# The third chunk's first layer norm regrouped through memory and turned by VectorE instead of TensorE

## The chip, the cores and the metric

The kernel runs on one core of a Trainium2 chip, in one launch. The metric is the device time of that core in microseconds (us). Times of a profile are counted from the start of the profiled span.

## The reference

The kernel computes one adaLN block over 2048 tokens of width 512, in float32: a linear attention with 32 heads of width 16, and a bilinear feed-forward of width 1376, each behind a layer norm that a condition vector scales and shifts.

```python
def _layernorm(x, eps=1e-5):
    m, v = mean(x, -1), var(x, -1)
    return (x - m) / jnp.sqrt(v + eps)

mod = (silu(c) @ w_mod)                      # six parts of 512: sa, ca, ga, sb, cb, gb
h = _layernorm(x) * (1 + ca) + sa
x = x + ga * A(h, wqkv, wo)
h = _layernorm(x) * (1 + cb) + sb
x = x + gb * (((h @ w_gate) * (h @ w_up)) @ w_down)

def A(x, wqkv, wo):
    q, k, v = heads(x @ wqkv)
    phi = lambda t: jnp.where(t > 0, t + 1, jnp.exp(t)) + 1e-6
    pq, pk = phi(q), phi(k)
    kv, z = sum_s(pk * v), sum_s(pk)         # per head: a 16 x 16 matrix and a vector
    return merge((pq @ kv) / (pq @ z + 1e-6)) @ wo
```

## The kernel before

A matrix product in float32 is made of three matmuls in a rounded format: each operand x is split into a high part h (a cast, on ACT) and a low part l = x - h (a subtraction, on DVE), and h*h, h*l and l*h are summed in PSUM. So each operand of a product costs a cast and a subtraction of a 128x512 tile.

The 2048 tokens are four chunks of four tiles of 128 tokens: tile i is tile j of chunk ch, i = 4 ch + j. The order of all instructions is written out by hand; each engine runs its own in that order, and semaphores make one engine wait for another. SBUF is a ring of 94 tiles of 128x512 (`B`), PSUM has four banks for accumulators (`acc_bank`) and four for work (`bank`). All DMAs are issued from the queue of SyncE (SP).

The first stage is the loop over i from 0 to 15 (L525 to L587). In step i, PE makes the keys of tile i + 2 (`proj(i + 2, wk)`, 12 matmuls), in the steps of `q_at` (i = 3, 4, 6, 7) also a query projection (`proj(..., wq)`, 12 matmuls) of one of the first four tiles, and the products of tile i's keys with its normalized tokens (`t_tile`, 12 matmuls into four accumulators). Beside that ACT and DVE split the normalized tile i + 1 (`k_split_x`) and its keys (`k_split`), apply phi to the keys of tile i + 2 (`k_phi`: two passes on ACT, one on DVE) and to the queries (`q_a`, `q_b`), and add up z (`z_add`).

The first layer norm of chunk ch + 1 (class `Norm`; `nx` in the loop) is spread over the steps of chunk ch and the end of the chunk before: the statistics of two tiles at j = 2 and two at j = 3 on DVE, the inverse deviation on POOL (`rstd_of`, a power) and `nmr_of` on DVE, then the scaled tile n on ACT (`xhat`; two tiles at j = 3, the others at j = 0 of the next chunk). At j = 0 and j = 1 of the chunk `turn_at` has `turn_x`: PE transposes the 128x128 blocks of the four tiles n into PSUM banks (L293, eight in each of the two steps), and `modulated` scales and shifts each bank on ACT (f, L305), casts it on DVE (L313) and subtracts (L316). The four pairs (h, l) of `norm[ch].t` are the left operands of the keys and queries of that chunk. For chunk 3 (index 2) this is in steps 4 and 5, and its first keys are made in step 6; for chunk 4 (index 3) it is in steps 8 and 9.

A second way to turn a tile is in use in later stages: a tile goes to DRAM and comes back with its 32x32 blocks regrouped, and DVE's transpose of 32x32 blocks does the rest. `move_out` and `move_in` do it for queries (one DMA out, four in, L723 and L731), `flip` and `flipped` for the second layer norm of the last two chunks, with the constant buffer `wide` between them (L901, L907).

The dictionary `extra` has the work on weights and modulation that is hung on the steps: the splits of the value weights in steps 4 to 7, the modulation from step 6 on, and the splits of the output weights `raw_o` in steps 12 and 13. Behind the loop come `den_z`, the scaling and splitting of the four accumulators (L655, L656, L660), and their product with the value weights (128x128 matmuls of `product` into `kvps`).

Of the kernel before, what the change touches and what calls it, by code (L numbers as in the profile page):

```python
# [8 lines left out]
F32 = mybir.dt.float32  # L9
F32R = mybir.dt.float32r  # L10
AF = mybir.ActivationFunctionType
ALU = mybir.AluOpType
AX = mybir.AxisListType

P = 128
NB = 94
BL = 32
NQ = P // BL
# [6 lines left out]
def tile_adaln_block(  # L25
# [42 lines left out]
    def f32(ap):  # L68
        return ap.bitcast(F32)
# [7 lines left out]
    def B(tag, shape=(P, D), dt=F32):  # L77

        return T(tiles, tag, shape, dt)
# [4 lines left out]
    def bank():  # L84
        return T(ps_w, "bank")
# [80 lines left out]
    def mod_col(acc, ps):  # L166

        for b in range(KD):
            nc.tensor.matmul(ps[:, b:b + 1], acc[:, b * P:(b + 1) * P], ones[:, 0:1], start=True, stop=True)
        return ps  # L170

    def col_out(v, ps, add):
        t = consts.tile([P, KD], F32, name=f"col{v}")
        nc.vector.tensor_scalar(t, ps[:, :KD], add, None, op0=ALU.add)
        return t
# [17 lines left out]
    def split(src, h, l, low=None):  # L193
        nc.scalar.activation(h, src, AF.Copy)  # L194
        (low or nc.vector).tensor_tensor(l, src, f32(h), op=ALU.subtract)  # L195

    def split_raw(raw, shape=(P, D), low=None):
        h = B("w", shape, F32R)
        l = B("w", shape, F32R)
        split(raw, h[:raw.shape[0]], l[:raw.shape[0]], low)  # L200
        return h, l
# [17 lines left out]
    def by_row(x):  # L219
        return x.rearrange("p (q s i) -> p s q i", q=NQ, i=BL)  # L220

    def split_blocks(raw):
        h, l = B("w", dt=F32R), B("w", dt=F32R)
        view = lambda x: x.rearrange("p (q s i) -> p q s i", q=NQ, i=BL)
        nc.scalar.activation(view(h), by_block(raw), AF.Copy)
        nc.vector.tensor_tensor(view(l), by_block(raw), view(f32(h)), op=ALU.subtract)
        return h, l
# [89 lines left out]
                self.t[k] = (h, l)  # L317


    NT = NCH * NJ  # L320
    norm = [Norm(xts[0])]
    wk, wq, wv = [], [], []
# [2 lines left out]
    def proj(i, w, of=bank):  # L325

        ch, j = divmod(i, NJ)
        ps = of()
        rows = w is wq and i not in FLIPPED
        product(ps.rearrange("p (s q i) -> p s q i", q=NQ, i=BL) if rows else ps,  # L330
                [(cut(norm[ch].t[k], j * P, (j + 1) * P), tuple(by_row(x) for x in w[k]) if rows else w[k])
                 for k in range(KD)])
        return ps
# [9 lines left out]
    def k_split_x(i):  # L343
        ch, j = divmod(i, NJ)
        kx[i] = [B("xh", dt=F32R), B("xl", dt=F32R)]
        split(norm[ch].n[j], *kx[i])

    def k_phi(i, ps):
        phi = B("phi")
# [11 lines left out]
    def k_split(i):  # L361
        h, l = B("kh", dt=F32R), B("kl", dt=F32R)
        phi = phk[i]
        nc.scalar.activation(h, phi, AF.Identity, bias=eps_phi)
        nc.vector.scalar_tensor_tensor(l, phi, EPS_PHI, f32(h), op0=ALU.add, op1=ALU.subtract)
        kx[i] += [h, l]

    def t_tile(i, *ks):
        xh, xl, kh, kl = kx[i]
        first, last = i == 0, i == NT - 1  # L370
        for k in ks:
            a, b = k * P, (k + 1) * P
            nc.tensor.matmul(tacc[k], xh[:, a:b], kh, start=first, stop=False)  # L373
            nc.tensor.matmul(tacc[k], xl[:, a:b], kh, start=False, stop=False)  # L374
            nc.tensor.matmul(tacc[k], xh[:, a:b], kl, start=False, stop=last)  # L375
# [6 lines left out]
    def q_b(i):  # L382
        phi_b(q_ps.pop(i), phq[i])
# [117 lines left out]
    def mod_load(*vs):  # L501
        raw_m.update({v: load_mod(v) for v in vs})

    def mod_part(v, *ks):
        if 0 in ks:
            accs[v] = B("f")
        mod_acc(accs[v], raw_m[v], ks)
# [6 lines left out]
             9: lambda: (mod_part(2, 2, 3), mod_load(4)),  # L514
             10: lambda: (pairs.update({2: split_raw(accs[2], low=nc.gpsimd)}), mod_part(3, 0, 1, 2), raw_o.extend(load(wo_v[k], "raw") for k in range(2))),
             11: lambda: (mod_part(3, 3), mod_part(4, 0, 1), rows.update({2: mod_row(2, pairs[2])}), raw_o.extend(load(wo_v[k], "raw") for k in range(2, KD))),
             12: lambda: (mod_part(4, 2, 3), wo_s.extend(split_raw(x) for x in raw_o[:2]), cols.update({3: col_out(3, mod_col(accs[3], bank()), 0.0)}), mod_load(5)),
             13: lambda: (mod_part(5, 0, 1, 2), wo_s.extend(split_raw(x) for x in raw_o[2:]), cols.update({4: col_out(4, mod_col(accs[4], bank()), 1.0)})),
             14: lambda: (mod_part(5, 3),)}
    pairs = {}  # L520
    q_at = {3: 0, 4: 1, 6: 2, 7: 3}
    ahead = {2: k_ps[2], 3: k_ps[3]}
    turn_at = {4 * ch + j: (ch + 1, 2 * j, 2 * j + 1) for ch in range(1, NCH - 1) for j in range(2)}
    turn_at.update({1: (1, 0, 1), 2: (1, 2, 3)})
    for i in range(NT):  # L525
        ch, j = divmod(i, NJ)
        done = 0
        if i > 2:
            ahead[i + 2] = proj(i + 2, wk) if i + 2 < NT else proj(i + 6 - NT, wq)
        if i in q_at:  # L530
            qps = proj(q_at[i], wq)
        def turn_x():
            to, *ks = turn_at[i]
            nx.transpose(*ks)
            nx.modulated(ca, sa, *ks, cast=nc.vector)
            norm[to:] = [nx]

        fresh = i > 0 and ch + 1 < NCH and j == 0
        if i == 2:
            turn_x()  # L540
            wq.extend(split_blocks(r) for r in raw_q)
        if fresh:
            nx.xhat(2)
        if 0 < i < NT - 1:
            k_split_x(i + 1)
        if fresh:
            nx.xhat(3)
        if 0 < i < NT - 1:
            k_split(i + 1)
        if i in turn_at and i != 2:  # L550
            t_tile(i, 0, 1)
            done = 2
            turn_x()
        if i == 2:
            t_tile(i, *range(KD))
            done = KD
            ahead[i + 2] = proj(i + 2, wk)
        if ch + 2 < NCH and j == 2:
            nx2 = Norm(xts[ch + 2])
            nx2.stats(0, 1)  # L560
        if ch + 2 < NCH and j == 3:
            nx = nx2
            nx.stats(2, 3)
            nx.rstd_of()
            nx.nmr_of()
            nx.xhat(0, 1)
        if i + 2 < NT:
            k_phi(i + 2, ahead.pop(i + 2))
        else:
            q_a(i + 6 - NT, ahead.pop(i + 2))  # L570
            q_b(i + 6 - NT)
        if i in q_at:
            q_a(q_at[i], qps)
            q_b(q_at[i])
        if i + 1 < NT:
            z_add(i + 1)
        if i == NT - 2:
            pairs["z"] = split_raw(zacc, low=nc.gpsimd)
        if i == NT - 1:
            zps = row_sum(pairs["z"])  # L580
            zb = consts.tile([P, D], F32, name="zb")
            nc.scalar.activation(zb, zps, AF.Identity, bias=eps_z)
            zq = B("z")
            nc.gpsimd.tensor_copy(zq.rearrange("p (q s i) -> p q s i", q=NQ, i=BL), by_block(zb))
        t_tile(i, *range(done, KD))
        if i in extra:
            extra[i]()  # L587
    ga, sb, cb = rows[2], cols[3], cols[4]
# [114 lines left out]
    def turn_h(i):  # L703
        pqs[i] = (B("xh", dt=F32R), B("xl", dt=F32R))
        nc.scalar.activation(pqs[i][0], tps[i], AF.Copy)
# [13 lines left out]
    def move_out(*tiles):  # L719

        for i in tiles:
            moved[i] = tc.dram_tile([P, D], F32, name=f"moved_{i}")
            nc.sync.dma_start(moved[i], phq.pop(i))  # L723

    def move_in(*tiles):

        for i in tiles:
            v = moved[i].rearrange("(m i) (q c) -> q i m c", i=BL, c=P)
            moved[i] = B("u")
            for q in range(NQ):  # L730
                nc.sync.dma_start(moved[i][q * BL:(q + 1) * BL].rearrange("i (m c) -> i m c", c=P), v[q])  # L731

    def turn_v(i):

# [19 lines left out]
    def y_seed(i, of=acc_bank):  # L754

        yps[i] = of()
        nc.scalar.activation(yps[i], xts[i // NJ][i % NJ], AF.Copy)
# [140 lines left out]

    def flip(ch, *js):
        for j in js:  # L900
            nc.vector.transpose(wide[:, j].rearrange("p (m s i) -> p m s i", m=NQ, i=BL),  # L901
                                blocks.pop((ch, j)).rearrange("p (m s i) -> p m s i", m=NQ, i=BL))

    def flipped(ch, *ks):
        for k in ks:
            f = B("f")
            nc.scalar.activation(f.rearrange("p (x i) -> p x i", i=BL),  # L907
                                 wide.rearrange("p j (m s i) -> p (j m) s i", m=NQ, i=BL)[:, :, k],
                                 AF.Identity, scale=cb[:, k:k + 1], bias=sb[:, k:k + 1])
            blocks[ch, "f", k] = f  # L910

    stowed, blocks = {}, {}

# [403 lines left out]
    first[0].sum("s1", "s3", on=nc.gpsimd)  # L1317
    g(lambda: turn_v(13))
    y_seed(13, y_bank)
    norm2[2].xhat_blocks(2, 3)  # L1320
    turn_h(13)
    turn_l(13)
    move_in(14, 15)
    stow(2, 0, 1, 2, 3)
# [107 lines left out]
```

## Time and profile before

| | |
|---|---|
| median of 3 runs | 554.86 us (554.34 to 554.95) |
| the profiled run | 554.37 us |
| its span | 552.7 us |
| granted TensorE clock | 1.000 |
| PE busy | 547.0 us (99%), 2488 matmuls |
| DVE busy | 373.6 us (68%) |
| ACT busy | 291.7 us (53%) |
| POOL busy | 203.4 us (37%) |
| DMA | 58.28 MB, mean 105 GB/s |

PE is the matmuls of TensorE, DVE is VectorE, ACT is ScalarE, POOL is GpSimd. A row of the timeline gives the start in us, the duration in us, the engine, the line of the kernel, the operation, out<-in by the program's names, the shapes and the count; in brackets stands the idle time ahead of it and what ended that. A row of the groups gives the line, engine, operation, names and shapes with their count, then the busy time in us and the mean ns of one, then the idle time before them. A row of the stretches gives the busy us of PE, the weight loads (PEld), DVE, ACT and POOL in turn, then the granted clock, the DMA share and GB/s.

### The profile page before, as it was taken

To read this page: it belongs to the slowest core of one execution; us is meant where nothing else is said; L and a number is where in the kernel's file an instruction comes from. 1 tells how busy PE (TensorE), PEld (TensorE's weight loads), DVE (VectorE), ACT (ScalarE), POOL (GpSimd) and SP (SyncE) were. 2 spreads that over 40 slices of the span, in tenths; PEclk is the share of its full clock that TensorE was granted. 3 is DMA by queue.
4 is the path that set the end of the run, shared out by engine and by line. 5 is a ranking of instruction groups with operands and counts; after the bars stand their busy time and mean duration, and the time that the engine had idled before them with its cause. 6 is when DMAs were issued, how large, how long until landed. Compare 5 with 4: busy or idle time off the path is not lost.

```text
span 552.7 us, 7324 instructions
## 1 busy us (share of the span) xinstructions
PE 547.0 (99%) x2488; PEld 449.2 (81%) x2488; DVE 373.6 (68%) x610; ACT 291.7 (53%) x539; POOL 203.4 (37%) x204
## 2 busy tenths in 40 slices
PE   8999999999999999999999999999999999999997
PEld 7788888888888878878888888877888888888886
DVE  7896968986887886778776576985444444434434
ACT  3695856646476667566684545454443444444110
POOL 2000000102003201057596666766666546446200
PEclk9999999999999999999999999999999999999999
DMA  8900203320503205845545071690434222200004
GB/s 284 387 15 2 76 20 103 108 77 1 157 2 133 96 5 186 267 145 135 160 111 155 0 230 38 216 322 2 133 116 132 59 57 59 58 20 0 1 0 152
DMA packets 58373, 58.28 MB, mean 105 GB/s; under 512 B 7328, under 2 KB 38304, under 8 KB 58336
## 3 DMA queue, kind: packets, MB, share of 16 engines
q1 hardware_dynamic: 58336, 57.83, 33.2%
q8 instruction: 19, 0.31, 0.2%
q14 instruction: 18, 0.15, 0.1%
HBM read 42.60 MB, written 15.20 MB: 105 GB/s over the span
## 4 chain that ended last, share of the span: by engine, by line
PE 99%; DVE 0%; issue 0%
PE bank L1030 33%; PE acc L766 7%; PE acc L1110 6%; PE acc L1111 6%; PE acc L1112 6%; PE bank L207 5%; PE bank L209 5%; PE bank L208 5%; PE acc L375 3%; PE acc L374 3%; PE acc L373 3%; PE bank L849 2%; PE bank L851 2%; PE bank L850 2%; PE acc L146 2%; PE bank L293 2%
## 5 line engine op out<-in xcount | busy, mean ns | idle before, releaser
L1030 PE MATMUL bank<-h,w 128*128 128x512 f32 (+1 forms) x798 | 184.7, 390 | 0.0
L1030 PEld LDWEIGHTS bank<-h,w 128*128 128x128 f32 (+1 forms) x798 | 148.4, 186 | 33.4 <-ACT bank L1035 0.7
L1035 ACT ACTIVATE bank<-bank 128x512 f32<-128x512 f32 (+1 forms) x38 | 22.2, 583 | 139.6 <-PE bank L1030 139.5
L836 DVE TENSOR_TENSOR x<-acc,x 128x512 f32<-128x512 f32 (+1 forms) x73 | 48.8, 682 | 48.4 <-PE acc L1112 47.7
L1016 POOL TENSOR_TENSOR w<-raw,w 128x256 fp32r<-128x256 f32 (+3 forms) x38 | 40.9, 1077 | 91.0 <-ACT w L1009 91.0
L1111 PE MATMUL acc<-w,kh 128*128 128x512 f32 (+2 forms) x154 | 59.6, 387 | 0.0
L1110 PE MATMUL acc<-w,kh 128*128 128x512 f32 (+2 forms) x154 | 59.6, 387 | 0.0
L1112 PE MATMUL acc<-w,kl 128*128 128x512 f32 (+2 forms) x154 | 59.5, 386 | 0.0
L263 POOL TENSOR_TENSOR rstd<-ve,half 128x4 f32<-128x4 f32 (+1 forms) x10 | 11.0, 1103 | 121.8 <-DVE ve L262 69.6
L195 POOL TENSOR_TENSOR w<-raw,w 128x512 fp32r<-128x512 f32 (+1 forms) x25 | 35.1, 1409 | 52.2 <-ACT w L194 47.3
L1016 POOL TENSOR_TENSOR w<-t,w 128x512 fp32r<-128x512 f32 (+1 forms) x38 | 49.2, 1318 | 0.0
L195 DVE TENSOR_TENSOR kl<-u,kh 128x512 fp32r<-128x512 f32 (+1 forms) x38 | 26.4, 736 | 30.6 <-ACT kh L194 30.6
L207 PE MATMUL bank<-w,h 128*128 128x512 f32 x104 | 40.9, 394 | 0.0
L209 PE MATMUL bank<-w,h 128*128 128x512 f32 x104 | 40.6, 391 | 0.0
L208 PE MATMUL bank<-w,h 128*128 128x512 f32 x104 | 40.6, 390 | 0.0
L766 PE MATMUL acc<-w,xh 128*128 128x512 f32 x120 | 37.4, 393 | 0.0
L1089 DVE TENSOR_TENSOR u<-bank,u 128x512 f32<-128x512 f32 (+1 forms) x19 | 13.1, 691 | 31.6 <-PE bank L1030 25.1
L1110 PEld LDWEIGHTS acc<-w,kh 128*128 128x128 f32 (+1 forms) x154 | 28.9, 188 | 6.0
L1112 PEld LDWEIGHTS acc<-w,kl 128*128 128x128 f32 (+1 forms) x154 | 28.9, 188 | 5.9
L1111 PEld LDWEIGHTS acc<-w,kh 128*128 128x128 f32 (+1 forms) x154 | 28.9, 188 | 5.9
L998 POOL TENSOR_TENSOR t<-raw,t 128x256 f32<-128x256 f32 (+1 forms) x34 | 25.9, 761 | 1.4
L766 PEld LDWEIGHTS acc<-w,xh 128*128 128x128 f32 x120 | 22.2, 188 | 4.6
(211 smaller groups left out, 1116.5 us busy)
## 6 DMA issues: line engine op xcount, KB each, us to landing
raw<-in_w_mod_dram SPq DMA_DIRECT2D x24, 256.0 KB, 3.7
raw<-in_B_w_down_dram SPq DMA_DIRECT2D x20, 256.0 KB, 3.2
raw<-in_B_w_gate_dram SPq DMA_DIRECT2D x36, 128.0 KB, 3.4
raw<-in_B_w_up_dram SPq DMA_DIRECT2D x36, 128.0 KB, 3.4
x<-in_A_x_dram SPq DMA_DIRECT2D x16, 256.0 KB, 5.4
out_dram<-x SPq DMA_DIRECT2D x15, 256.0 KB, 2.6
raw<-in_A_wqkv_dram SPq DMA_DIRECT2D x12, 256.0 KB, 5.4
moved<-h SPq DMA_DIRECT2D x12, 256.0 KB, 2.1
```

The lines of the kernel that those rows point to most:

```text
L195: (low or nc.vector).tensor_tensor(l, src, f32(h), op=ALU.subtract)
L207: nc.tensor.matmul(ps, ah, bh, start=i == 0, stop=False)
L208: nc.tensor.matmul(ps, ah, bl, start=False, stop=False)
L209: nc.tensor.matmul(ps, al, bh, start=False, stop=i == n - 1)
L766: nc.tensor.matmul(yps[i], x, y, start=False, stop=k == KD - 1 and x is al, skip_group_check=True)
L836: nc.vector.tensor_tensor(xt[:, a:b], dn[j][:, a:b], xt[:, a:b], op=ALU.add)
L998: sub = lambda out, x, y: (on or nc.gpsimd).tensor_tensor(out, x, y, op=ALU.subtract)
L1016: sub = lambda out, x, y: (on or nc.gpsimd).tensor_tensor(out, x, f32(y), op=ALU.subtract)
L1030: mm = lambda x, y, **kw: nc.tensor.matmul(ps, x[:, k], y, skip_group_check=True, **kw)
L1110: nc.tensor.matmul(ps, hh[:, a:b], dh[:n, c:d], start=i == 0, stop=False)
L1111: nc.tensor.matmul(ps, hh[:, a:b], dl[:n, c:d], start=False, stop=False)
L1112: nc.tensor.matmul(ps, hl[:, a:b], dh[:n, c:d], start=False, stop=i == len(hs) - 1)
```

## The change

For chunk 3 alone (`LIFTED = (2,)`) the 16 transposes on PE go. Its statistics, `nmr` and scaled tiles n are made in pairs, all by the end of step 3, with the columns of n grouped in blocks (`xhat_blocks`). Each n goes to DRAM (`lift_out`, one DMA) and back regrouped (`lift_in`, four DMAs), DVE turns it into `wide` (`lift_turn`: two tiles at the end of step 4, two in step 5), ACT scales and shifts four rows out of `wide` (`lift_row`), and the parts are made by `lift_parts`, the cast on ACT for rows 0 and 2 and on DVE for rows 1 and 3. `k_split_x` reads that chunk's n through a permuting pattern. In step 6 the query projection goes ahead of the keys of tile 8, the first that need chunk 3. The splits of the output weights move from steps 12 and 13 to steps 14 and 15. In a later stage `turn_h(13)` goes ahead of two scaled tiles of the second norm. `move_out`, `move_in`, `flip` and `flipped` call the new helpers and do the same as before.

```diff
+    LIFTED = (2,)
+
+    def lift_out(name, x):
+        to = tc.dram_tile([P, D], F32, name=name)
+        nc.sync.dma_start(to, x)
+        return to
+
+    def lift_in(of):
+        v = of.rearrange("(m i) (q c) -> q i m c", i=BL, c=P)
+        u = B("u")
+        for q in range(NQ):
+            nc.sync.dma_start(u[q * BL:(q + 1) * BL].rearrange("i (m c) -> i m c", c=P), v[q])
+        return u
+
+    def lift_turn(j, u):
+        nc.vector.transpose(wide[:, j].rearrange("p (m s i) -> p m s i", m=NQ, i=BL),
+                            u.rearrange("p (m s i) -> p m s i", m=NQ, i=BL))
+
+    def lift_row(k, scale, shift):
+        f = B("f")
+        nc.scalar.activation(f.rearrange("p (x i) -> p x i", i=BL),
+                             wide.rearrange("p j (m s i) -> p (j m) s i", m=NQ, i=BL)[:, :, k],
+                             AF.Identity, scale=scale[:, k:k + 1], bias=shift[:, k:k + 1])
+        return f
+
+    def lift_parts(k, f, cast=True):
+        h, l = B("h", dt=F32R), B("h", dt=F32R)
+        if k % 2 and cast:
+            nc.vector.tensor_copy(h, f)
+        else:
+            nc.scalar.activation(h, f, AF.Copy)
+        nc.vector.tensor_tensor(l, f, f32(h), op=ALU.subtract)
+        return h, l
...
-        split(norm[ch].n[j], *kx[i])
+        if ch not in LIFTED:
+            split(norm[ch].n[j], *kx[i])
+            return
+        x = by_row(norm[ch].n[j])
+        h, l = (t.rearrange("p (s q i) -> p s q i", q=NQ, i=BL) for t in kx[i])
+        nc.scalar.activation(h, x, AF.Copy)
+        nc.vector.tensor_tensor(l, x, f32(h), op=ALU.subtract)
...
-             12: lambda: (mod_part(4, 2, 3), wo_s.extend(split_raw(x) for x in raw_o[:2]), ...
-             13: lambda: (mod_part(5, 0, 1, 2), wo_s.extend(split_raw(x) for x in raw_o[2:]), ...
-             14: lambda: (mod_part(5, 3),)}
+             12: lambda: (mod_part(4, 2, 3), ...
+             13: lambda: (mod_part(5, 0, 1, 2), ...
+             14: lambda: (mod_part(5, 3), wo_s.extend(split_raw(x) for x in raw_o[:2])),
+             15: lambda: wo_s.extend(split_raw(x) for x in raw_o[2:])}
...
-    turn_at = {4 * ch + j: (ch + 1, 2 * j, 2 * j + 1) for ch in range(1, NCH - 1) for j in range(2)}
-    turn_at.update({1: (1, 0, 1), 2: (1, 2, 3)})
+    turn_at = {1: (1, 0, 1), 2: (1, 2, 3), 8: (3, 0, 1), 9: (3, 2, 3)}
     for i in range(NT):
         ch, j = divmod(i, NJ)
         done = 0
+        up = ch + 1 if ch + 1 in LIFTED else None
+        far = ch + 2 if ch + 2 in LIFTED else None
+        if i == 6:
+            qps = proj(q_at[i], wq)
         if i > 2:
             ahead[i + 2] = proj(i + 2, wk) if i + 2 < NT else proj(i + 6 - NT, wq)
-        if i in q_at:
+        if i in q_at and i != 6:
             qps = proj(q_at[i], wq)
...
+        if far and j == 3:
+            nx = nx2
+            nx.nmr_of(0, 2)
+            nx.xhat_blocks(0, 1)
+            lifts = [lift_out(f"first_{ch}_{n}", nx.n[n]) for n in range(2)]
+        fresh = i > 0 and ch + 1 < NCH and not up and j == 0
...
         if 0 < i < NT - 1:
             k_split(i + 1)
+        if up and j == 1:
+            lift_turn(2, lifts[2])
+            lift_turn(3, lifts[3])
+            for k in range(KD):
+                nx.t[k] = lift_parts(k, lift_row(k, ca, sa))
+            norm[up:] = [nx]
...
             nx2.stats(0, 1)
+            if far:
+                nx2.rstd_of(0, 2)
...
             nx.stats(2, 3)
-            nx.rstd_of()
-            nx.nmr_of()
-            nx.xhat(0, 1)
+            nx.rstd_of(*((2, 4) if far else ()))
+            if not far:
+                nx.nmr_of()
+                nx.xhat(0, 1)
...
             q_b(q_at[i])
+        if far and j == 3:
+            nx.nmr_of(2, 4)
+            nx.xhat_blocks(2, 3)
+            lifts[0], lifts[1] = lift_in(lifts[0]), lift_in(lifts[1])
+            lifts += [lift_out(f"first_{ch}_{n}", nx.n[n]) for n in (2, 3)]
+            lifts[2], lifts[3] = lift_in(lifts[2]), lift_in(lifts[3])
...
         t_tile(i, *range(done, KD))
+        if up and j == 0:
+            lift_turn(0, lifts[0])
+            lift_turn(1, lifts[1])
...
+    turn_h(13)
     norm2[2].xhat_blocks(2, 3)
-    turn_h(13)
     turn_l(13)
```

More of the change, by code (lines that the diff above doesn't have):

```diff
@@ L516, in tile_adaln_block @@
              11: lambda: (mod_part(3, 3), mod_part(4, 0, 1), rows.update({2: mod_row(2, pairs[2])}), raw_o.extend(load(wo_v[k], "raw") for k in range(2, KD))),
-             12: lambda: (mod_part(4, 2, 3), wo_s.extend(split_raw(x) for x in raw_o[:2]), cols.update({3: col_out(3, mod_col(accs[3], bank()), 0.0)}), mod_load(5)),
-             13: lambda: (mod_part(5, 0, 1, 2), wo_s.extend(split_raw(x) for x in raw_o[2:]), cols.update({4: col_out(4, mod_col(accs[4], bank()), 1.0)})),
-             14: lambda: (mod_part(5, 3),)}
+             12: lambda: (mod_part(4, 2, 3), cols.update({3: col_out(3, mod_col(accs[3], bank()), 0.0)}), mod_load(5)),
+             13: lambda: (mod_part(5, 0, 1, 2), cols.update({4: col_out(4, mod_col(accs[4], bank()), 1.0)})),
+             14: lambda: (mod_part(5, 3), wo_s.extend(split_raw(x) for x in raw_o[:2])),
+             15: lambda: wo_s.extend(split_raw(x) for x in raw_o[2:])}
     pairs = {}
@@ L536, in turn_x @@
             norm[to:] = [nx]
-        fresh = i > 0 and ch + 1 < NCH and j == 0
         if i == 2:
@@ L721, in move_out @@
         for i in tiles:
-            moved[i] = tc.dram_tile([P, D], F32, name=f"moved_{i}")
-            nc.sync.dma_start(moved[i], phq.pop(i))
+            moved[i] = lift_out(f"moved_{i}", phq.pop(i))
     def move_in(*tiles):
         for i in tiles:
[L728 to L731, printed above, removed]
+            moved[i] = lift_in(moved[i])
     def turn_v(i):
@@ L900, in flip @@
         for j in js:
-            nc.vector.transpose(wide[:, j].rearrange("p (m s i) -> p m s i", m=NQ, i=BL),
-                                blocks.pop((ch, j)).rearrange("p (m s i) -> p m s i", m=NQ, i=BL))
+            lift_turn(j, blocks.pop((ch, j)))
     def flipped(ch, *ks):
         for k in ks:
[L906 to L910, printed above, removed]
+            blocks[ch, "f", k] = lift_row(k, cb, sb)
     stowed, blocks = {}, {}
```

## The prediction

> **What bounds the kernel now.** I read the page first: the busy shares and the chain that ended last.
>
> ```profile
> span 552.7 us, 7324 instructions
> PE 547.0 (99%) x2488; PEld 449.2 (81%) x2488; DVE 373.6 (68%) x610; ACT 291.7 (53%) x539; POOL 203.4 (37%) x204
> PE 99%; DVE 0%; issue 0%
> ```
>
> TensorE is the path from end to end, so an edit counts only by the matmul time that it takes away and by the pauses that it makes. The profiled run took 554.37 us, 1.67 more than its span and 0.49 below the median of 554.86; I add the change to both. What a measurement can tell from no change is about 0.2%, here 1.1 us. Next I read the busy times by stretch over the loop steps i = 4 and i = 6.
>
> ```profile
> 48.90:58.00 9.10, 9.10 (x45) 7.57 (x44) 4.20 (x8) 7.79 (x13) 1.01 (x1) 1.00 0.00 0
> 64.40:72.70 8.30, 8.30 (x38) 6.78 (x37) 7.81 (x16) 6.51 (x12) 0.00 (x0) 1.00 0.20 63
> ```
>
> The third pair of numbers is DVE, the fourth ACT. PE never rests, but DVE is full (7.81 of 8.30 us) just behind the place where the change puts work on it.
>
> **What goes: 16 PE transposes.** They stand in i = 4 and i = 5, in the timeline of PE:
>
> ```profile
> 55.79 1.03 PE L293 MATMUL bank<-ident,n 128*128 128x128 f32 x8
> 56.90 0.39 PE L374 MATMUL acc<-kh,xl 128*128 128x512 f32 x1
> 62.14 1.03 PE L293 MATMUL bank<-ident,n 128*128 128x128 f32 x8
> 63.24 0.40 PE L374 MATMUL acc<-kh,xl 128*128 128x512 f32 x1
> 64.39 0.39 PE L207 MATMUL bank<-w,h 128*128 128x512 f32 x1
> 67.11 0.40 PE L207 MATMUL bank<-w,h 128*128 128x512 f32 x1
> 69.91 0.39 PE L373 MATMUL acc<-kh,xh 128*128 128x512 f32 x1
> 85.03 1.04 PE L293 MATMUL bank<-ident,n 128*128 128x128 f32 x8
> ```
>
> A 128x512 matmul takes 0.227 us (67.11 - 64.39 over 12). From the first transpose to the second matmul behind them are 1.11 and 1.10 us, of which one matmul is 0.23: the two groups cost 0.88 + 0.87 = 1.76 us of path. That is the whole gain, if PE waits for nothing new. A 128x128 block costs PE 0.11 us here; on DVE a tile of four blocks takes 0.70 (below), 0.17 a block, and then is turned only within 32x32 blocks. The Trainium skill ("VectorE: DVE Perf Modes", The three transpose paths) gives 390 ns for one on TensorE and 311 ns on VectorE, and sends a full 128x128 to TensorE. By its 390 ns the 16 would be worth an estimated 6.2 us; in this trace they are pipelined, and the rows decide.
>
> **What comes: the same tiles through memory and DVE.** I walk ACT and DVE by hand from the last instruction that both kernels share in time, the statistics of chunk 3 (norm[2]) at 42.85.
>
> ```profile
> 42.85 0.68 DVE L242 BATCH_NORM_STATS2 st<-x 128x6 f32<-128x512 f32 x1
> 44.46 0.66 DVE L341 SCALAR_TENSOR_TENSOR phi<-bank,phi 128x512 f32<-128x512 f32 x1
> 48.57 0.17 DVE L262 TENSOR_SCALAR ve<-mv 128x4 f32<-128x4 f32 x1
> 48.91 1.01 POOL L263 TENSOR_TENSOR rstd<-ve,half 128x4 f32<-128x4 f32 x1 [19.53 <-DVE ve L262]
> 49.95 0.16 DVE L267 SCALAR_TENSOR_TENSOR nmr<-mv,rstd 128x4 f32<-128x4 f32 x1 [1.21 <-POOL rstd L263]
> 50.15 1.52 ACT L272 ACTIVATE n<-x,nmr,rstd 128x512 f32<-128x512 f32 x2 [4.27 <-DVE nmr L267]
> 51.58 0.58 ACT L337 ACTIVATE phi<-bank 128x512 f32<-128x512 f32 x1
> 52.19 0.63 ACT L338 ACTIVATE phi<-phi 128x512 f32<-128x512 f32 x1
> 52.72 0.58 ACT L337 ACTIVATE h<-bank 128x512 f32<-128x512 f32 x1
> L194 ACT ACTIVATE w<-raw 128x512 fp32r<-128x512 f32 x36 | 22.0, 623 | 0.8 <-DMA raw<-in_A_wqkv_dram 0.8
> L907 ACT ACTIVATE f<-wide,col,col 128x512 f32<-128x512 f32 x8 | 6.4, 806 | 0.0
> L313 DVE CAST h<-f 128x512 fp32r<-128x512 f32 x19 | 8.5, 449 | 5.5 <-ACT f L305 5.5
> L901 DVE STREAM_TRANSPOSE wide<-u 128x512 f32<-128x512 f32 x8 | 5.5, 699 | 0.0
> ```
>
> These rows give the rules: an instruction that waits starts some 0.04 after its releaser's end, one that doesn't starts 0.09 before its predecessor's end, a pair of statistics takes 1.61 (42.85 to 44.46), and from `ve` to `xhat` pass 1.58 us (48.57 to 50.15), POOL's power included.
>
> Step i = 3. Statistics 0 and 1 end at 44.54, so `ve` comes at 44.58 and ACT's xhat 0 and 1 at 46.15. ACT then runs xh, kh, phi, exp, h, exp to 51.1. DVE's statistics 2 and 3 follow its kl at 49.45, `ve` at 51.18, xhat 2 and 3 at 52.75, to 54.27. Behind them ACT has xh, kh of tile 5 and the four phi passes of i = 4, until 57.7. DVE takes up that h at 57.75 and has eight more in its order: z, turn 0, turn 1, the first wv split, xl, kl, turn 2, turn 3, at 0.60 each: the last turn ends at 63.28. The data is there before:
>
> ```profile
> moved<-h SPq DMA_DIRECT2D x12, 256.0 KB, 2.1
> 173.70 1.82 SPq L731 DMA_DIRECT2D u<-moved  x4
> u<-moved SPq DMA_DIRECT2D x48, 64.0 KB, 2.0
> ```
>
> xhat 3 leaves at 54.3 and lands at 56.4; SP issues its four reads at 0.46 us each behind the four of tile 2, from 57.4, and the last lands near 61, 1.6 us before DVE comes to it. The 20 added DMAs are all issued by 59.3. The loads behind them on SP, for the modulation's third part, are not held up: from 48.90 to 58.00 nothing was moved before (DMA share 0.00 in the row above).
>
> Step i = 5. ACT and DVE now alternate: row 0 from 63.32 (0.81), its cast on ACT, row 1, row 2, cast 2, row 3 ending at 67.57; DVE has l0 at 64.82, then cast 1, l1, l2, cast 3, l3, to 68.77. PE comes to i = 6 at 64.39 - 1.76 = 62.63, spends 2.80 on the q projection that now stands ahead (69.91 - 67.11), and starts the keys of tile 8 at 65.43; their last matmul would start at 67.93, but l3 is there at 68.8. That pause is 0.9 us. It alone would leave a gain of 0.9. The q projection is the cover here: without it the pause were 3.7.
>
> **What is late next.** DVE works in order, so everything behind l3 starts late as well, and at its end stands chunk 4's norm.
>
> ```profile
> 65.11 0.69 DVE L316 TENSOR_TENSOR h<-f,h 128x512 fp32r<-128x512 f32 x1
> 65.72 0.68 DVE L341 SCALAR_TENSOR_TENSOR phi<-bank,phi 128x512 f32<-128x512 f32 x1
> 71.40 0.69 DVE L341 SCALAR_TENSOR_TENSOR h<-bank,h 128x512 f32<-128x512 f32 x1 [0.38 <-ACT h L338]
> 76.15 0.17 DVE L262 TENSOR_SCALAR ve<-mv 128x4 f32<-128x4 f32 x1
> 77.53 0.16 DVE L267 SCALAR_TENSOR_TENSOR nmr<-mv,rstd 128x4 f32<-128x4 f32 x1 [1.21 <-POOL rstd L263]
> 83.21 0.80 ACT L272 ACTIVATE n<-x,nmr,rstd 128x512 f32<-128x512 f32 x1
> ```
>
> Before, the phi behind the last l starts at 65.72; now at 68.77, 3.05 later. From there to `ve` at 76.15 DVE has the same list in both kernels and rests only 0.38 us, which the earlier q projection removes: `ve` and `nmr` come 2.67 late. From `nmr` to the end of xhat 3 (77.53 to 84.01) ACT's list is the same, so chunk 4's last n is there at 86.68. PE's fourth transpose of i = 8, the first to read it, stood at 85.03 + 0.30 = 85.33, which left 1.32 us of slack. Now it starts at 86.72: 1.39 later than before. PE reaches it with all of the 1.76 won and 0.9 lost again; the pause there, 2.3 us, eats the rest. So the sum up to here is lag minus slack, +1.39, whatever the first pause was.
>
> **Output weights.** The splits in steps 14 and 15 replace those in 12 and 13. The pair of step 14 fits into DVE's 3.49 us of rest. The pair of step 15 stands ahead of the next chain:
>
> ```profile
> 127.45 0.69 DVE L341 SCALAR_TENSOR_TENSOR h<-bank,h 128x512 f32<-128x512 f32 x1 [3.49 <-ACT h L338]
> 129.07 2.73 DVE L656 SCALAR_TENSOR_TENSOR n<-zb,col,n 128x512 f32<-128x512 f32 x4
> 131.73 2.49 DVE L195 TENSOR_TENSOR w<-n,w 128x512 fp32r<-128x512 f32 x4
> 134.59 0.22 PE L207 MATMUL bank<-w,w 128*128 128x128 f32 x1
> ```
>
> Two casts on ACT (1.06) and two subtractions on DVE, the first at 128.56: the four n start 1.71 later, at 130.78, and the last low part ends at 135.93 in place of 134.22. PE needs it for the eleventh of its 128x128 matmuls, at 134.59 + 10 x 0.11 = 135.7: +0.3. Bounds: nothing, if DVE is a little ahead, and 0.6.
>
> **Edits at nothing.** The permuted read of chunk 3's n in the key split costs what a plain one does: a strided split of the same size took ACT 0.632 against 0.623 for the plain one above.
>
> ```profile
> L225 ACT ACTIVATE w<-raw 128x512 fp32r<-128x512 f32 x4 | 2.2, 632 | 0.0
> ```
>
> `turn_h(13)` ahead of two xhat passes moves 0.62 us on ACT at a place where PE waits for nothing; the passes feed stores read much later. If that cover failed it would cost 0.6.
>
> **Sum.** +1.39 + 0.3 = +1.7: 556.1 for a profiled run like this one, 556.5 us against the median.
>
> **The rivals.** Faster (0.10): DVE catches up. Below a lag of 1.0 us the sum is negative; with no lag it is -1.32 at best, since the slack was only 1.32 while PE came 1.76 earlier: 553.5. It speaks for it that DVE has idle time before (4.20 of 9.10 us in i = 4); against it, that this idle time stands ahead of the h at 57.75, for which DVE waits in either case. Turns 0 and 1 done in that rest would give 1.2 back, but the written order has them behind z.
>
> No change that can be told (0.18): the lag is 0.7 to 2.1 and the sum -0.3 to +1.1, since my rules add 0.04 at each of a dozen handovers, the alternation of rows and casts may run 0.5 tighter, and the output weights may cost nothing; 555.4.
>
> Later still (0.06): the tiles' reads land late. The slack is 1.6 us; if 16 more reads took 2 us more each, as loads in a queue can, the last turn moves by 0.5 to 2 and the sum with it: 557.5 and more. Also here: PE's clock. Granted is 1.00 in every stretch quoted, so no row shows a pause's effect; were half of the next 3 us lost, it were +1.5. The Trainium skill ("TensorE: Matmul & The Clock Gate", Part 1) has the clock halved after an idle window of about 3.4 us; by that rule neither pause is long enough.
>
> **Numbers.** The forecast, 0.66, is 556.5. The range is 554.4 to 557.8: below are the faster rival, above the tail of the late reads. Slower by over 0.2%: 0.66 + 0.06, less 0.02 for a small plus = 0.70; within: 0.20; faster: 0.10.
>
> **What would show it.** Right: no PE transposes between i = 3 and i = 8; a pause of some 0.9 us in the keys of tile 8, PE waiting for DVE's h; `nmr` of chunk 4 some 2.7 us after 77.53; a pause of some 2 us within the eight transposes of i = 8, PE waiting for ACT's n; 0.3 before the 128x128 matmuls. Wrong: PE without a pause in i = 6 and i = 8, or a last turn that ends before 61.5.

## The result, and the profile after

The changed kernel takes 556.12 us in the median (555.48 to 557.37, 9 runs), the kernel before 554.95 us (554.34 to 555.67, 9 runs): a ratio of 1.0026, 95% interval 1.0015 to 1.0036. That is 1.4 us slower (0.8 to 2.0), by the ratio times 554.95.

First the page of the kernel after: the span, the busy times, and the chain that ended last.

```profile
span 554.4 us, 7346 instructions
PE 547.2 (99%) x2472; PEld 447.8 (81%) x2472; DVE 377.1 (68%) x614; ACT 292.8 (53%) x541; POOL 203.6 (37%) x205
PE 94%; DVE 3%; ACT 2%; issue 1%; POOL 0%; POOLq 0%; DVEq 0%
```

The 16 matmuls are gone (2488 to 2472) and yet PE is no less busy. It rests 1.5 us more (554.4 less 547.2, against 552.7 less 547.0), and a pause of a few tenths counts as busy, in matmuls that last longer. The chain shows where: it was 99% PE, now 5% of it lies on DVE and ACT (that is the stretch over which it runs on them, not the time lost). The same chain, in order of time (start us, us, what), tells where it leaves PE:

```profile
68.79 0.50 PE bank L209
69.33 0.68 DVE z L399
...
77.84 0.59 DVE st L242
79.01 1.02 POOL rstd L263
80.25 1.52 ACT n L272 x2
...
85.81 0.71 ACT n L272
86.57 0.77 PE bank L293 x5
```

It leaves in the keys of tile 8, in step 6, runs through DVE's list to the last statistics of chunk 4, over POOL's power to ACT's scaled tiles, and comes back to PE in the transposes of step 8. That is the path of "what is late next" in the prediction. The timeline of DVE and ACT has the two ends of it:

```profile
68.03 0.69 DVE L352 TENSOR_TENSOR h<-f,h 128x512 fp32r<-128x512 f32 x1
68.72 0.69 DVE L376 SCALAR_TENSOR_TENSOR phi<-bank,phi 128x512 f32<-128x512 f32 x1
78.67 0.17 DVE L262 TENSOR_SCALAR ve<-mv 128x4 f32<-128x4 f32 x1
80.05 0.16 DVE L267 SCALAR_TENSOR_TENSOR nmr<-mv,rstd 128x4 f32<-128x4 f32 x1 [1.21 <-POOL rstd L263]
85.72 0.80 ACT L272 ACTIVATE n<-x,nmr,rstd 128x512 f32<-128x512 f32 x1
```

And the timeline of PE at the three places where it pauses: in the keys of tile 8 (rows of 0.50 where 0.40 is usual, with starts up to 0.45 apart in place of 0.23), in the transposes of step 8, and in the 128x128 matmuls behind the loop.

```profile
67.61 0.50 PE L209 MATMUL bank<-w,h 128*128 128x512 f32 x1
68.06 0.50 PE L207 MATMUL bank<-w,h 128*128 128x512 f32 x1
68.78 0.50 PE L209 MATMUL bank<-w,h 128*128 128x512 f32 x1
69.11 0.40 PE L414 MATMUL acc<-kh,xh 128*128 128x512 f32 x1
84.25 0.38 PE L293 MATMUL bank<-ident,n 128*128 128x128 f32 x2
85.34 0.33 PE L293 MATMUL bank<-ident,n 128*128 128x128 f32 x1 [0.71 <-ACT n L272]
86.57 0.77 PE L293 MATMUL bank<-ident,n 128*128 128x128 f32 x5 [0.90 <-ACT n L272]
137.24 0.33 PE L208 MATMUL bank<-w,w 128*128 128x128 f32 x1
```

The last of the late key matmuls starts at 68.78, 0.06 after the last low part of chunk 3 is done on DVE (68.03 + 0.69 = 68.72): that is what the end of the pause in step 6 waits for.

The cleanest reading is the shift: the start of one and the same matmul in this profile less its start in the profile of before. At 50 us, ahead of everything that the change does to PE, it stands at +0.23, from the start of the run:

```profile
50.48 0.39 PE L207 MATMUL bank<-w,h 128*128 128x512 f32 x1
```

against the same matmul of before:

```profile
50.25 0.39 PE L207 MATMUL bank<-w,h 128*128 128x512 f32 x1
```

All shifts below are less that of their own run at 50 us, so they hold the loop and what follows, and not the first stage, which differs from one execution to the next. An example: the transposes of step 8 began at 85.03 before and at 84.25 after, -0.78, less 0.23 is -1.01. Shift in us, worked out from the timelines of PE:

| kernel | ahead of step 6 | ahead of step 8 | behind step 8 | behind the 128x128 matmuls | end |
|---|---|---|---|---|---|
| after | -1.78 | -1.01 | +1.04 | +1.40 | +1.52 |
| e1: chunk 4's statistics ahead of the rows | -1.78 | -1.02 | -1.02 | -0.65 | -0.61 |
| e2: output weights back | -1.78 | -1.03 | +1.05 | +1.05 | +1.03 |
| e3: q projection back | -1.78 | +1.77 | +1.77 | +2.13 | +2.09 |
| e4: 16 PE transposes added | 0.00 | 0.00 | +1.02 | +1.38 | +1.41 |
| e5: e1 and e2 | -1.78 | -1.02 | -1.02 | -1.02 | -1.05 |
| e6: e5 and earlier turns | -1.78 | -1.78 | -1.78 | -1.81 | -1.57 |
| e7: before, statistics moved | 0.00 | +1.02 | +1.02 | +1.02 | +1.01 |

The row of "after" is the account: 1.78 won, 0.77 lost in step 6, 2.05 lost in step 8, 0.36 at the output weights, 0.12 later (near 222 us; see "Edits at nothing" below).

### The profile page after: what moved, and what is told of

Its sections match the earlier page's. It is cut to its first block, busy times and chain, and to the rows that moved or that the text cites. A ratio compares the mean times of both kernels' runs of the same rounds, so it can differ in the third digit from the quotient of the medians.

```text
span 554.4 us, 7346 instructions
## 1 busy us (share of the span) xinstructions
PE 547.2 (99%) x2472; PEld 447.8 (81%) x2472; DVE 377.1 (68%) x614; ACT 292.8 (53%) x541; POOL 203.6 (37%) x205
## 4 chain that ended last, share of the span: by engine, by line
PE 94%; DVE 3%; ACT 2%; issue 1%; POOL 0%; POOLq 0%; DVEq 0%
PE bank L1089 33%; PE acc L830 7%; PE acc L1169 6%; PE acc L1170 6%; PE acc L1171 6%; PE bank L209 4%; PE bank L207 4%; PE bank L208 4%; PE acc L416 2%; PE acc L415 2%; PE acc L414 2%; PE acc L146 2%; PE bank L913 2%; PE bank L915 2%; PE bank L914 2%; PE bank L293 1%
## 5 line engine op out<-in xcount | busy, mean ns | idle before, releaser
L263 POOL TENSOR_TENSOR rstd<-ve,half 128x2 f32<-128x2 f32 (+1 forms) x11 | 11.3, 1032 | 124.1 <-DVE ve L262 71.2
```

## The experiments

Theory: DVE, which works in order, ends the parts of chunk 3 late; its list hands that lag to chunk 4's norm, and PE waits for it in step 8, so that the sum there is lag less slack whatever PE won before. Rivals: the loss is the pause in step 6 alone, or lies in what the reads and DMAs do to others, or the transposes of PE were worth nothing. All times were taken beside runs of the kernel before; a ratio is to that.

**e1: chunk 4's statistics ahead of the rows.** The lag is left as it is, but not handed on: the statistics of chunk 4 stand in steps 4 and 5 instead of 6 and 7.

```diff
+        if up and j == 0:
+            nx3 = Norm(xts[ch + 2])
+            nx3.stats(0, 1)
...
             lift_turn(3, lifts[3])
+            nx3.stats(2, 3)
+            nx3.rstd_of()
...
-            nx2 = Norm(xts[ch + 2])
-            nx2.stats(0, 1)
+            nx2 = nx3 if up else Norm(xts[ch + 2])
+            if not up:
+                nx2.stats(0, 1)
...
-            nx.stats(2, 3)
-            nx.rstd_of(*((2, 4) if far else ()))
+            if not up:
+                nx.stats(2, 3)
+                nx.rstd_of(*((2, 4) if far else ()))
```

> The changed kernel, but chunk 4's statistics are made in two holes of DVE: tiles 0 and 1 at the head of step 4, tiles 2 and 3 (and the power on POOL) in step 5 between turn 3 and the first low part, where DVE waited 1.55 us for ACT. Theory of the lag (DVE's order makes chunk 4's norm late, and that sets the time): the two pauses of PE in the transposes of step 8 (1.6 us by the waits, some 2.0 of shift) go, the pause in the keys of tile 8 grows by 0.1 to 0.4, and the span is 1.6 to 2.0 us below the changed kernel's 554.4, that is 552.4 to 552.8, near that of before (552.7). Rival (the pause in step 8 comes from ACT's own list of phi passes and splits, not from DVE's statistics): the pause stays within 0.3 us and so does the span.

Measured: 554.16 us, ratio 0.9991 (0.9981 to 1.0). The timeline of DVE, ACT and PE:

```profile
75.81 0.15 DVE L267 SCALAR_TENSOR_TENSOR nmr<-mv,rstd 128x4 f32<-128x4 f32 x1
81.46 0.80 ACT L272 ACTIVATE n<-x,nmr,rstd 128x512 f32<-128x512 f32 x1
84.35 1.03 PE L293 MATMUL bank<-ident,n 128*128 128x128 f32 x8
```

The last n starts 4.26 us earlier than in the kernel after (81.46 against 85.72), the eight transposes run as one row without a pause, and the shift stays at -1.02 across step 8. So the 2.05 us there hung on the statistics behind the late list: with these moved, nothing else holds PE back in step 8. The pause in step 6 had been expected to grow by 0.1 to 0.4; it stays at 0.76 (-1.78 to -1.02).

**e2: output weights back** in steps 12 and 13.

```diff
-             12: lambda: (mod_part(4, 2, 3), cols.update(...
-             14: lambda: (mod_part(5, 3), wo_s.extend(split_raw(x) for x in raw_o[:2])),
-             15: lambda: wo_s.extend(split_raw(x) for x in raw_o[2:])}
+             12: lambda: (mod_part(4, 2, 3), wo_s.extend(split_raw(x) for x in raw_o[:2]), cols.update(...
+             13: lambda: (mod_part(5, 0, 1, 2), wo_s.extend(split_raw(x) for x in raw_o[2:]), ...
+             14: lambda: (mod_part(5, 3),)}
```

> The changed kernel with the splits of the output weights back in steps 12 and 13. Theory (the pair in step 15 delays the chain to the 128x128 matmuls): the shift of 0.38 us there goes, nothing else moves, span 0.3 to 0.4 below 554.4. Rival (DVE is so late after the turned chunk that steps 12 and 13 have no room any more): a new pause between steps 12 and 15 takes back 0.3 or more, span 554.4 or above.

Measured: 555.83 us, ratio 1.0021 (1.0011 to 1.0031). The times of e2 and of the changed kernel (1.0015 to 1.0036) can't be told apart; the trace can. Up to step 8 both have the same shifts, and at the 128x128 matmuls e2's stays at +1.05 where the other's goes from +1.04 to +1.40. The later splits cost 0.36 us.

**e3: the q projection behind the keys of tile 8 again.**

```diff
-        if i == 6:
-            qps = proj(q_at[i], wq)
...
-        if i in q_at and i != 6:
+        if i in q_at:
             qps = proj(q_at[i], wq)
```

> The changed kernel with the query projection of step 6 behind the keys of tile 8 again, so that the 2.80 us of cover are gone. Theory of the lag (time = the later of PE's own way and chunk 4's norm): the pause in the keys of tile 8 grows from 0.75 to some 3.5 us, but the pause in step 8, 2.0 us, goes; the span grows by 0.6 to 1.0, to 555.0 to 555.4. Rival (each pause is paid for itself): the pause in step 8 stays and the span grows by 2.8, to 557.2.

Measured: 557.62 us, ratio 1.0047 (1.003 to 1.0064). The timeline of PE at the first key:

```profile
64.27 0.50 PE L207 MATMUL bank<-w,h 128*128 128x512 f32 x1 [1.81 <-ACT h L351]
```

PE waits 1.8 us for the first h, then for each later part. In all the keys cost 3.55 us of shift (-1.78 to +1.77) in place of 0.77, and step 8 then costs nothing. By the trace the end is only 0.57 us later than with the projection ahead (2.09 against 1.52): of the 2.78 us that the cover is worth in step 6, step 8 takes 2.05 when it is there. The timed difference is larger, 2.6 us against before, and its interval wide (+1.7 to +3.6). Three of the six runs have a mean granted clock of 0.992 or 0.993 and took 558.0 to 558.5 us; the two at 1.000 took 556.14 and 557.04. So the median holds lost clock as well as pauses. A loss in both places, -1.78 + 3.55 + 2.05 + 0.36 + 0.12 = +4.3, is outside the interval all the same.

**e4: the 16 transposes put back on PE** as work that nobody reads, eight in step 4 and eight in step 5; all else as in the changed kernel.

```diff
+        if up and j < 2:
+            t_tile(i, 0, 1)
+            done = 2
+            for _ in range(2):
+                ps = bank()
+                for b in range(NJ):
+                    nc.tensor.transpose(ps[:, b * P:(b + 1) * P], ident, ident)
```

> The changed kernel with 16 transposes put back on PE in steps 4 and 5, of a constant into banks that nobody reads: PE does the work that the change took away, all else is as in the changed kernel. Theory of the lag: PE comes 1.76 us later to step 6 and 8, the pauses there shrink by as much (0.75 to nothing, 2.0 to some 1.2 or less), and the span stays at 554.4 within 0.2: the gain from taking the transposes off PE is worth nothing in this order. Rival (the gain is real and the pauses are paid on top): the span grows by 1.76, to 556.1.

Measured: 556.54 us, ratio 1.0025 (1.0016 to 1.0034). PE's transposes of step 8:

```profile
86.06 0.77 PE L293 MATMUL bank<-ident,n 128*128 128x128 f32 x5 [0.80 <-ACT n L272]
```

PE gets 1.78 us more to do and the time is the same (1.0025 against 1.0026). The pause in step 6 is gone, that in step 8 is half as long, and behind step 8 the shift is +1.02 against +1.04. This shows "lag minus slack" most plainly: in the changed kernel the matmuls taken from PE earn nothing, because PE meets the same n at the same time with them and without: the last five transposes of step 8 start at 86.57 - 0.23 = 86.34 without them and at 86.06 + 0.28 = 86.34 with them, where 0.23 and -0.28 are the two runs' shifts at 50 us.

**e5: e1 and e2 together**, with the edits shown there.

> Chunk 4's statistics in DVE's holes (as e1) and the output weights' splits back in steps 12 and 13 (as e2). If lag and output weights are separate terms, the sum of both: against before, from step 3 on, -1.78 for the transposes, +0.77 for the pause in the keys of tile 8, nothing in step 8, nothing at the 128x128 matmuls: -1.0 us, ratio 0.998. Rival (with the statistics early, steps 12 and 13 are too full on DVE, as the reason for moving the splits may have been): a pause there of 0.3 or more, total -0.7 or above.

Measured: 553.83 us, ratio 0.9977 (0.9965 to 0.9988), 1.3 us faster than before; by the trace -1.05. The two repairs add up: 1.04 + 1.02 at step 8 and 0.36 at the weights.

**e6: e5, and turns 0 and 1 in DVE's rest.** In e5 the pause of step 6 is left. In the kernel after DVE rests twice in step 4, waiting for ACT's phi passes, and the first two turns stand behind that:

```profile
56.59 0.69 DVE L376 SCALAR_TENSOR_TENSOR phi<-bank,phi 128x512 f32<-128x512 f32 x1 [0.45 <-ACT phi L373]
57.74 0.69 DVE L376 SCALAR_TENSOR_TENSOR h<-bank,h 128x512 f32<-128x512 f32 x1 [0.46 <-ACT h L373]
58.95 1.30 DVE L336 STREAM_TRANSPOSE wide<-u 128x512 f32<-128x512 f32 x2
61.94 1.29 DVE L336 STREAM_TRANSPOSE wide<-u 128x512 f32<-128x512 f32 x2
```

```diff
+        if up and j == 0:
+            lift_turn(0, lifts[0])
         if i + 2 < NT:
             k_phi(i + 2, ahead.pop(i + 2))
+            if up and j == 0:
+                lift_turn(1, lifts[1])
...
-        if up and j == 0:
-            lift_turn(0, lifts[0])
-            lift_turn(1, lifts[1])
```

> As e5, and the turns of tiles 0 and 1 stand ahead of the two phi passes of DVE in step 4, where DVE waited for ACT (0.45 and 0.46 us in the changed kernel), in place of behind z. Theory (the pause in the keys of tile 8 comes from DVE's list ahead of the last turn, not from the reads out of memory): the last turn ends about 1 us earlier, near 62.2, the pause of 0.77 us goes, and the total against before is the whole gain of the transposes, -1.6 to -1.8 us, ratio 0.997. Rival (the alternation of rows, casts and subtractions, or the data's landing, sets it): the pause stays at 0.5 to 0.8 and the total at -1.0.

Measured: 553.17 us, ratio 0.9968 (0.9955 to 0.9981): 1.8 us faster than before, and faster than both kernels of this case. The timeline of DVE:

```profile
57.48 0.70 DVE L336 STREAM_TRANSPOSE wide<-u 128x512 f32<-128x512 f32 x1
58.11 0.65 DVE L376 SCALAR_TENSOR_TENSOR phi<-bank,phi 128x512 f32<-128x512 f32 x1
58.69 0.69 DVE L336 STREAM_TRANSPOSE wide<-u 128x512 f32<-128x512 f32 x1
59.30 0.66 DVE L376 SCALAR_TENSOR_TENSOR h<-bank,h 128x512 f32<-128x512 f32 x1
62.27 1.30 DVE L336 STREAM_TRANSPOSE wide<-u 128x512 f32<-128x512 f32 x2
```

Neither phi waits now (no bracket), the turns lie in what was rest. This run stands at +1.66 at 50 us where the kernel after has +0.23, so the last pair starts at 62.27 - 1.43 = 60.84 on the other's clock, 1.10 earlier than its 61.94. The pause of 0.77 is gone, and the shift is -1.78 ahead of step 8 and behind it: all that the transposes cost is won, and -1.57 of it is left at the end. All 20 added DMAs are still there, so they are not what the kernel after loses by. The earlier turns were not tried without the edits of e1 and e2.

**e7, a control: the kernel before with chunk 4's statistics in steps 4 and 5.** It shows whether e1 gains because that place is a better one anyway.

```diff
+        if ch + 2 == NCH - 1 and j == 0:
+            nx3 = Norm(xts[ch + 2])
+            nx3.stats(0, 1)
+        if ch + 2 == NCH - 1 and j == 1:
+            nx3.stats(2, 3)
+            nx3.rstd_of()
...
-            nx2 = Norm(xts[ch + 2])
-            nx2.stats(0, 1)
+            nx2 = nx3 if ch else Norm(xts[ch + 2])
+            if not ch:
+                nx2.stats(0, 1)
...
-            nx.stats(2, 3)
-            nx.rstd_of()
+            if not ch:
+                nx.stats(2, 3)
+                nx.rstd_of()
```

> The kernel before (transposes on PE) with chunk 4's statistics moved to the same places as in e1, steps 4 and 5. Theory (the early statistics help only because the changed kernel has holes on DVE there; in the kernel before chunk 4's norm has slack and step 5 is full): no gain, and a new pause in the keys of tile 8 of 0.5 to 1.3 us, because 1.6 us of statistics stand ahead of the casts and subtractions of chunk 3: +0.5 to +1.3 against before. Rival (early statistics are a gain by themselves and e1's -2 was theirs): -0.5 or more against before.

Measured: 555.45 us, ratio 1.0006 (0.9996 to 1.0017), no difference that can be told. In the timeline of DVE the statistics stand ahead of the parts of chunk 3:

```profile
62.39 0.68 DVE L242 BATCH_NORM_STATS2 st<-x 128x6 f32<-128x512 f32 x1
66.92 0.69 DVE L316 TENSOR_TENSOR h<-f,h 128x512 fp32r<-128x512 f32 x1
```

The last of those parts, at 65.11 before, starts at 66.92, PE pauses in the keys of tile 8, and by the trace the end is 1.01 later, just above the interval's +0.94. The place gains nothing by itself: in the kernel before it is the worse one.

## Why the prediction was right

The forecast was 1.7 us slower; it is 1.4 by the times and 1.52 by the shift. The mechanism was the one forecast: the pauses are where it put them and wait for what it named, and that says more than the range, 554.4 to 557.8, which would have held no change as well. The term of the sum that was mis-sized is the lag, by 0.35. That the total is off by less has some luck in it: 0.06 more at the output weights and 0.12 later, which the sum didn't hold, made up half.

**What goes.** 1.76 was said, 1.78 measured; and that it is real gain only if PE waits for nothing new is what e4 and e6 show, from both sides. The 390 ns that the prediction took from the Trainium skill ("VectorE: DVE Perf Modes", The three transpose paths) stand there for a transpose in bf16; in this float32 kernel the 16 were worth 0.11 us each.

**The walk of DVE and ACT.** The last turn was to end at 63.28, it ends at 63.23; the last l was to end at 68.77, it ends at 68.72. The profile after is 0.23 later in itself, so the walk was about 0.28 too slow. Some 0.2 of that was there by xhat 2 and 3 already: 52.75 was said, they start here:

```profile
52.76 1.52 ACT L279 ACTIVATE n<-x,nmr,rstd 128x512 f32<-128x512 f32 x2 [1.55 <-DVE nmr L267]
```

From there to the last l the walk lost only some 0.07 more. The pause in step 6 is 0.77 where 0.9 was said, and e3 shows the pause without the cover, 3.55 where 3.7 was said.

**The reads.** They were to be in time with 1.6 us of slack. The third turn starts at 61.94 with no wait in its row, so they were, and the rival of late reads is out. SP's queue, by its timeline:

```profile
55.73 3.64 SPq L332 DMA_DIRECT2D u<-first  x8
```

The last reads are issued by 59.37, as said, and the modulation's loads follow from 60.28.

**What is late next.** This is the term that decided, and the one mis-sized most. The lag of `nmr` was put at 2.67; it is 80.05 - 77.53 = 2.52, less 0.23 is 2.29. So the sum is +1.04 where +1.39 was said. Of the 0.38 of lag, 0.28 came with the walk and 0.10 behind it, between phi and `ve`, and most of it has two causes. The walk counted 1.57 us from `ve` to xhat both times, with POOL's power at 1.01, which is the price of four columns; on two columns the power takes 0.70 (rows in the last section), and from `ve` to xhat pass 1.46 (44.80 to 46.26) and 1.47 (51.29 to 52.76). That is 0.21 or so, not twice 0.31, since `nmr` then waited for DVE's pass ahead of it. And the rest of 0.38 us on DVE that went was worth 0.47, because the next pass now starts before its predecessor's end, as the prediction's own rule of 0.09 has it. The timeline of DVE before and, below it, after:

```profile
70.34 0.67 DVE L341 SCALAR_TENSOR_TENSOR phi<-bank,phi 128x512 f32<-128x512 f32 x1
71.40 0.69 DVE L341 SCALAR_TENSOR_TENSOR h<-bank,h 128x512 f32<-128x512 f32 x1 [0.38 <-ACT h L338]
```

```profile
73.35 0.67 DVE L376 SCALAR_TENSOR_TENSOR phi<-bank,phi 128x512 f32<-128x512 f32 x1
73.94 0.68 DVE L376 SCALAR_TENSOR_TENSOR h<-bank,h 128x512 f32<-128x512 f32 x1
```

From phi to h were 1.06 us and are 0.59. So the error was not the one that the prediction named as a doubt, 0.04 at each of a dozen handovers. The slack of 1.32 was right to within 0.1: 2.29 less 1.04 is 1.25.

One clause was too broad: that the sum holds "whatever the first pause was". It holds while the pause in step 6 is shorter than what PE has in hand. With e3's 3.55 PE itself comes later than n, and the first pause alone sets +1.77.

**Output weights.** +0.3 was said, 0.36 measured (e2). The four n were to start at 130.78 and start at 132.04, and the 128x128 matmuls at 135.86 in place of 134.59: 1.26 and 1.27 later, so against PE the walk of DVE was right.

```profile
132.04 2.73 DVE L724 SCALAR_TENSOR_TENSOR n<-zb,col,n 128x512 f32<-128x512 f32 x4
135.86 0.22 PE L207 MATMUL bank<-w,w 128*128 128x128 f32 x1
```

**Edits at nothing.** The permuted reads are made in steps 7 to 10, and in e2, which has them, the shift is +1.05 behind step 8 and +1.05 behind the 128x128 matmuls. `turn_h(13)` lies near 250 us, and the shift of the kernel after does not move from there on. So both cost nothing that the traces show. The 0.12 arises near 222 us, where PE takes up a low part that DVE has late, behind a turn that waited 0.39 us for its read out of memory. In e6 a wait of 0.47 costs as much at the same place; in the other five runs with these edits nothing is lost there. Whether the change makes these reads later is open.

**The rivals.** "Faster, 553.5" needed DVE to have no lag. Its remark that turns 0 and 1 done in DVE's rest "would give 1.2 back" came out at 1.10 in e6; it takes e1's move and e2's as well to be 1.8 us faster. The granted clock of the kernel after was 1.00 through both pauses, in the stretches of step 6 and of step 8:

```profile
64.40:72.70 8.30, 8.30 (x34) 5.98 (x34) 7.56 (x14) 8.17 (x15) 0.00 (x0) 1.00 0.08 29
81.00:89.00 8.00, 6.39 (x32) 5.00 (x31) 4.99 (x9) 7.91 (x15) 0.00 (x0) 1.00 0.44 132
```

The rule of the Trainium skill that the prediction named ("TensorE: Matmul & The Clock Gate", Part 1: half the clock after an idle window of about 3.4 us) fits here: no wait of PE in the kernel after is longer than 0.90 us from 50 us on. In the profiled run of e3, where one lasts 1.81, the clock stayed at 1.00 too. The three runs of e3 with a mean clock of 0.992 or 0.993 have no profile, so whether that pause can cost clock is open.

## What to carry to other kernels

Work that is moved from the engine that sets the time to one that has rest pays only if it is done in that rest: ask which instruction of the in-order list each rest waits for, and put the new work ahead of that one, not behind it. Follow the lag to the end of the list, past the first consumer: here the first pause took 0.77 us and was covered by a projection, and the statistics for the chunk after, far down the same list, took 2.05. And compare lag with slack before counting the gain: where the lag is larger, the work saved ahead of it earns nothing, as 16 transposes showed that were put back, read by nobody, and cost nothing.

## What the runs showed of the hardware

POOL's power on 128x2 takes 0.70 us, where the one on 128x4 takes 1.01 in the same run; the prediction had counted 1.01 for each:

```profile
51.54 0.69 POOL L263 TENSOR_TENSOR rstd<-ve,half 128x2 f32<-128x2 f32 x1 [5.70 <-DVE ve L262]
79.01 1.01 POOL L263 TENSOR_TENSOR rstd<-ve,half 128x4 f32<-128x4 f32 x1 [26.77 <-DVE ve L262]
```

In the first stage, which no edit touches, the granted clock can fall to half. In two profiled runs it did, after pauses no longer than those of steps 6 and 8. By the stretches of e6:

```profile
16.00:17.00 1.00, 1.00 (x6) 0.91 (x6) 0.68 (x4) 1.00 (x2) 0.00 (x0) 0.63 1.01 356
17.00:18.00 1.00, 1.00 (x3) 0.72 (x3) 0.62 (x2) 1.00 (x3) 0.00 (x0) 0.50 1.07 365
18.00:19.00 1.00, 1.00 (x4) 0.79 (x3) 1.00 (x3) 1.00 (x3) 0.00 (x0) 0.50 0.98 346
19.00:20.00 1.00, 1.00 (x5) 0.78 (x4) 0.97 (x3) 1.00 (x3) 0.00 (x0) 0.67 1.04 393
```

In stretches of 0.1 us the clock reads 0.50 from 16.3 to 19.6 in e6 and from 16.7 to 20.0 in e5, with one mixed value at each end and 1.00 outside: some 3.4 us at half speed, which loses 1.7. That is about what e5 and e6 stand at by 50 us (+1.38 and +1.66), so their spans (553.0 and 552.7 us) say less than their shifts. In both runs PE had waited in the 7 us ahead of it, 0.47 us at once in e5 and up to 0.57 in e6:

```profile
13.63 0.66 PE L300 MATMUL bank<-ident,n 128*128 128x128 f32 x4 [0.57 <-ACT n L272]
```

That these waits are the cause is not shown: e1 waited there too, up to 0.63 us at once (4.21 us busy of the 5.00 from 9 to 14 us, e6 4.15), and kept 1.00. The same page of the Trainium skill ("TensorE: Matmul & The Clock Gate", Part 1) has a window of 3.4 us that runs freely, so that the point of a change varies from run to run. The 3.4 us at half clock agree with it; that waits of half a microsecond should be enough does not follow from its idle window.
